# Queries and keys laid out before the launch, three half-height products per score, a shorter weight conversion, and new durations in the plan

## The chip, the cores and the metric

The kernel runs on one core of one Trainium2 chip. The metric is the device time of one execution in microseconds: the median of 3 runs is 1234.06 us (1233.96 to 1236.8). The core has five engines that run beside each other, each in the order of its own queue: TensorE (PE in the rows, its weight loads PEld), VectorE (DVE), ScalarE (ACT), GpSimd (POOL) and SyncE (SP), which here only issues DMA transfers.

## The reference, cut to what matters

```python
def _attn_ref(q, k, v):            # (4, 8, 576, 64) each: batch, heads, rows, width
    scores = scale * np.matmul(q, k.transpose(0, 1, 3, 2))
    kth = np.partition(scores, -32, axis=-1)[..., -32:-31]
    scores = np.where(scores >= kth, scores, -1e9)     # only the 32 largest of a row stay
    attn = softmax(scores)
    return np.matmul(attn, v)
x = attn_out.transpose(0, 2, 1, 3).reshape(2304, 512)
x = ((x @ w_a) * (x @ w_b)) @ w_out                    # 512 -> 1536 -> 512, "MoE 1" in the code
logits = x @ w_gate                                    # 8 experts
out[rows of expert e] = gate[:, None] * (np.maximum(x @ w1[e], 0) @ w2[e])   # each row to one expert
```

`w_a`, `w_b` and `w_out` arrive as 8-byte floats; everything else has 4 bytes.

## The kernel before

The kernel has three parts that overlap. Attention runs over 4 batches and 4 pairs of heads. Batch 0 is taken in two halves of its rows (320 and 256 of the 576), so it has 8 units (pair, half); batches 1 to 3 have 4 units each, 12 in all, the "later units". The feed-forward `moe1` follows for each half or batch, and after the last batch the 8 experts.

**Units.** `load_unit` brings q, k and v of one unit in, rows on partitions, and `prep_unit` turns q and k so that the head's 64 columns lie on partitions. In batch 0 (`u.f`) the turned operands stay f32: TensorE transposes at L488 and L491, ScalarE copies out of PSUM at L498 to L503, and a score (L597, and L572 for the last 64 rows of both heads) is an f32 matmul per head with 64 rows of contraction. In the later units q and k are first split into two float32r parts, a rounded one and the rest (ScalarE at L512, GpSimd at L514). The two parts of one head lie on 64 partitions each, so that one matmul of 128 rows computes high by high plus low by low, and a second one with a copy of k whose halves are swapped (`kS`, a transfer of 304 KB in two issues at L542) the mixed products. The turning is 18 transposes a unit at L523 and copies at L528 to L540. A score over one chunk of 128 rows and half of the keys has two heads by two products (L601); the score of the last 64 rows of both heads has eight matmuls (L578).

**Selection.** ScalarE copies half of the scores out of PSUM (L606), VectorE takes the larger and the smaller of the two halves (`m`, `n`, L614), and finds the 32 largest by rounds of MAX8 and MATCH_REPLACE8 (L625 to L652). ScalarE does the exponentials (L633), VectorE masks and sums (L680), TensorE turns the result (L706, L715) and multiplies it by v (L727, L731).

**Conversion.** `conv` makes a 4-byte float out of each 8-byte one by arithmetic on its two words, in 36 pieces of 128 x 512: ScalarE L387 (magnitude), VectorE L389 (shift and mask), ScalarE L391 (sign), VectorE L392 (shift and or), GpSimd L395 (times the sign). `split` (L400, L401) then makes two float32r parts, and these go to DRAM (`ws`, `wos`), from where `moe1` reads them (L824, L854: three products each). The first two pieces are loaded at once; the others wait for `U[0].mark`, which was the last copy of the first unit's preparation.

**Order.** Nothing is issued in program order. `Plan` holds each operation with an engine, a reckoned duration and a position `pos`; `emit` simulates the engines with these durations and issues each engine's operations in the order in which the simulation started them, the ready one with the smallest `pos` first. Attention has small positions, `moe1` large ones, so feed-forward matmuls fill TensorE where attention leaves it free. The durations are the functions `c_act`, `c_dve`, `c_ts`, `c_pool`, `c_mm` and `c_dma` and some numbers at the call. SP issues the loads and stores in the plan's order too.

Of the kernel before, what the change touches and what calls it, by code (L numbers as in the profile page):

```python
# [13 lines left out]
U32 = mybir.dt.uint32  # L14
AF = mybir.ActivationFunctionType
# [181 lines left out]
def c_pool(n):  # L197
    return 150 + n * 2.1


def c_mm(n, k=1):
    return k * (max(n, 256) / 2.4 + 2.5)
# [7 lines left out]
def fused_kernel(ctx: ExitStack, tc: tile.TileContext, q, k, v, w_a, w_b, w_out, w_gate, w1, w2, out,  # L210
                 opts=None, dbg=None):
    nc = tc.nc
# [18 lines left out]
    HALVES = opts.get("halves", (0,))  # L231
    FU = opts.get("fu", range(8))
# [74 lines left out]
    qm_t, rr_t = [], []  # L307
    for i in range(2):
        qm_t.append(cst.tile([128, 192], F32R, name=f"qm{i}"))
        nc.gpsimd.memset(fr(qm_t[i]), 0.0)  # L310
    for i in range(opts.get("rr", 1)):
        rr_t.append(cst.tile([128, 5, 128], F32, name=f"rr{i}"))
        nc.gpsimd.memset(rr_t[i], 0.0)
    id2 = cst.tile([128, 64], F32, name="id2")
# [14 lines left out]
    QM = [P_.fixed(t) for t in qm_t]  # L329
# [27 lines left out]
    def conv_bufs():  # L357
# [74 lines left out]
    def load_unit(ui, b, p, groups, pos, after=None):  # L432
        u = Rec()
        u.b, u.p, u.f, u.first = b, p, ui in FU, ui == 0
        ch = [x - x // 3 for g in groups for x in GT[g] if x != 2]
        u.c = min(ch), max(ch) + 1, any(2 in GT[g] for g in groups)
        h0 = 2 * p
# [6 lines left out]
        for nm, src in (("k", k), ("q", q)):  # L444
            z = T(p_at, [128, 10, 64], F32, "raw" + nm, opts.get("raw", 1))
            u.raw[nm] = z
            if u.f:
                a, e, last = u.c if nm == "q" else (0, 4, True)
                for h in range(2):
                    load(c_dma(65536 * (e - a)), pos, lambda z=z, h=h, a=a, e=e: z()[:, h + 2 * a:h + 2 * e - 1:2, :],  # L450
                         src[b, h0 + h, 0:512, :].rearrange("(p c) d -> p c d", c=4)[:, a:e], [(z, h)])
                if last:
                    load(c_dma(65536), pos, lambda z=z: z()[0:64, 8:10, :],
                         src[b, h0:h0 + 2, 512:576, :].rearrange("h s d -> s h d"), [(z, 2)])
                continue
            load(c_dma(262144), pos, lambda z=z: z()[:, 0:8, :].rearrange("p (h c) d -> p h c d", h=2),
                 src[b, h0:h0 + 2, 0:512, :].rearrange("h (p c) d -> p h c d", c=4), [(z, 0)])
            for h in range(2):
                load(c_dma(16384), pos, lambda z=z, h=h: z()[64 * h:64 * h + 64, 8, :], src[b, h0 + h, 512:576, :],
                     [(z, 1 + h)])  # L460
        z = T(p_at, [128, 2, 5, 64], F32, "vt", opts.get("vt", 2))
        vp = 40 if u.first else pos + 1
        load(c_dma(262144), vp, lambda: z()[:, :, 0:4, :],
             v[b, h0:h0 + 2, 0:512, :].rearrange("h (p c) d -> p h c d", c=4), [(z, 0)])
        for h in range(2):
            load(c_dma(16384), vp, lambda h=h: z()[64 * h:64 * h + 64, h, 4, :], v[b, h0 + h, 512:576, :], [(z, 1 + h)])
        u.vt = z
        return u

    def prep_unit(u, i, pos, step):  # L470
        u.qm, u.rr = QM[i % 2], RR[i % len(RR)]
# [1114 lines left out]
```

## Time and profile before

| | |
|---|---|
| median of 3 runs | 1234.06 us |
| profiled execution, its time | 1233.15 us |
| its span, first to last instruction | 1231.4 us |
| PE busy | 1103.6 us, 90%, 7710 matmuls |
| PEld busy | 981.2 us, 80% |
| DVE busy | 896.3 us, 73%, 2636 instructions |
| ACT busy | 718.1 us, 58%, 1567 |
| POOL busy | 460.6 us, 37%, 622 |
| DMA moved | 215.49 MB in 116863 packets, 28883 of them under 512 B |

Busy is the time in which an engine had an instruction in it. Matmuls are pipelined: a row's duration holds the time to fill and empty the array, and what a matmul costs in a stream is the distance from its start to the next one's start. Rows that follow each other with the same line and shape are merged in the timeline, with their count.

### The profile page before, as it was taken

How to read it: one execution, taken by the hardware profiler on the slowest of the kernel's cores; microseconds unless marked ns; L12 is line 12 of the kernel's file. 1: busy time of each engine (PE TensorE's matmuls, PEld its weight loads, DVE VectorE, ACT ScalarE, POOL GpSimd, SP SyncE). 2: the span in 40 equal slices, each digit the busy share in tenths (PEclk: the TensorE clock that was granted, in tenths of full speed). 3: DMA queues.
4: the chain of work that ended last, by engine and by line, in shares of the span. 5: the costliest groups of instructions: out<-in, count | busy, mean ns of one | idle time of the engine just before them, and what ended most of it. 6: DMA issues, size and time to landing. Idle time of an engine off the chain costs nothing.

```text
span 1231.4 us, 22514 instructions
## 1 busy us (share of the span) xinstructions
PE 1103.6 (90%) x7710; PEld 981.2 (80%) x7710; DVE 896.3 (73%) x2636; ACT 718.1 (58%) x1567; POOL 460.6 (37%) x622
## 2 busy tenths in 40 slices
PE   4656796979999789999999999999999999999996
PEld 2333474868888579889888998989999899999996
DVE  6999999999998999999998999910004545444441
ACT  6667676776667567666765766633224445544551
POOL 3455566755536234234535422455234100000001
PEclk9966798989999999999999999999899999999998
DMA  8487578999677234244243442246535655554450
GB/s 235 130 276 229 164 245 261 323 303 300 208 255 248 93 87 144 109 153 144 78 152 112 132 151 104 86 155 225 191 147 184 189 152 174 176 177 151 159 177 22
DMA packets 116863, 215.49 MB, mean 175 GB/s; under 512 B 28883, under 2 KB 77011, under 8 KB 109061
## 3 DMA queue, kind: packets, MB, share of 16 engines
q1 hardware_dynamic: 113525, 204.52, 52.4%
q0 software_dynamic: 3216, 9.46, 2.0%
q8 instruction: 63, 1.03, 0.4%
q14 instruction: 59, 0.48, 0.1%
HBM read 171.82 MB, written 35.25 MB: 168 GB/s over the span
## 4 chain that ended last, share of the span: by engine, by line
PE 55%; DVE 14%; DMA 11%; issue 8%; ACT 7%; POOL 4%; SPq 1%; POOLq 0%; ACTq 0%; DVEq 0%
PE ab L824 16%; PE ab L854 9%; PE ab L1182 5%; PE pv L727 5%; DVE am L680 3%; DVE m L638 3%; PE ms L1231 3%; PE pv L1231 3%; PE sp L601 3%; DVE kt L641 2%; PE tp L706 2%; DMA xsort<-rows,pi 2%; DMA rawk<-in_k_dram 2%; DMA wt<-wos 1%; PE pv L731 1%
## 5 line engine op out<-in xcount | busy, mean ns | idle before, releaser
L824 PE MATMUL ab<-xh,wt 128*128 128x320 f32 (+1 forms) x1344 | 303.9, 304 | 3.9 <-ACT sb L809 3.8
L824 PEld LDWEIGHTS ab<-xh,wt 128*128 128x128 f32 x1344 | 227.6, 191 | 13.2 <-issue 7.8
L824 PE MATMUL ab<-xl,wt 128*128 128x320 f32 (+1 forms) x672 | 199.9, 297 | 0.0
L638 DVE MATCH_REPLACE8 m<-kt,m 128x288 f32<-128x288 f32 x432 | 188.5, 440 | 0.0
L641 DVE MAX8 kt<-m 128x8 f32<-128x288 f32 x432 | 182.3, 444 | 0.5
L854 PE MATMUL ab<-gH,wt 128*128 128x320 f32 (+1 forms) x768 | 171.8, 305 | 4.5 <-DMA wt<-wos 4.5
L680 DVE SCALAR_TENSOR_TENSOR am<-s,kt,e 128x576 f32<-128x576 f32 x144 | 139.8, 996 | 0.3
L854 PEld LDWEIGHTS ab<-gH,wt 128*128 128x128 f32 x768 | 130.7, 193 | 6.7 <-DMA wt<-wos 3.9
L832 POOL TENSOR_TENSOR sa<-sa,sb 128x320 f32<-128x320 f32 (+1 forms) x96 | 79.6, 829 | 145.0 <-ACT sb L809 144.5
L824 PEld LDWEIGHTS ab<-xl,wt 128*128 128x128 f32 x672 | 128.8, 192 | 0.0
L633 ACT ACTIVATE e<-s,nm 128x576 f32<-128x576 f32 x144 | 108.6, 778 | 11.6 <-POOL nm L628 11.3
L854 PE MATMUL ab<-gT,wt 128*128 128x320 f32 (+1 forms) x384 | 115.1, 300 | 0.0
L1256 POOL DMA_INDIRECT out_dram<-y,ti x23 | 23.0, 999 | 227.6 <-ACT y L1250 212.6
L1100 DVE TENSOR_TENSOR wp<-raw,wp 128x1024 fp32r<-128x1024 f32 (+1 forms) x73 | 67.4, 942 | 55.6 <-ACT wp L1099 55.2
L606 ACT COPY s<-sp 128x576 f32<-128x576 f32 x128 | 81.9, 640 | 42.9 <-PE sp L601 23.7
L706 PE MATMUL tp<-idr,am 128*128 128x128 f32 x512 | 84.8, 304 | 20.3 <-ACT aT L710 7.2
L401 POOL TENSOR_TENSOR gT<-sa,gH 128x320 fp32r<-128x320 f32 (+1 forms) x96 | 84.6, 881 | 45.8 <-ACT gH L400 45.4
L706 PEld LDWEIGHTS tp<-idr,am 128*128 128x128 f32 x512 | 64.1, 155 | 38.6 <-ACT aT L710 15.8
L1182 PE MATMUL ab<-xgh,wp 128*128 128x304 f32 (+6 forms) x352 | 89.4, 312 | 1.1 <-DVE gT L1189 0.7
L710 ACT COPY aT<-tp 128x512 f32<-128x512 f32 x128 | 72.4, 587 | 26.6 <-PE tp L706 25.8
L727 PE MATMUL pv<-aT,vt 128*64 128x320 f32 (+1 forms) x512 | 79.2, 451 | 6.5 <-ACT aT L695 4.5
L809 ACT ACTIVATE sa<-ab 128x320 f32<-128x320 f32 (+1 forms) x120 | 49.4, 412 | 53.9 <-PE ab L824 30.7
(303 smaller groups left out, 2560.8 us busy)
## 6 DMA issues: line engine op xcount, KB each, us to landing
wt<-ws SPq DMA_DIRECT2D x54, 1024.0 KB, 5.6
wt<-wos SPq DMA_DIRECT2D x44, 768.0 KB, 5.7
raw<-in_moe_w_dram SPq DMA_DIRECT2D x64, 512.0 KB, 3.7
kS<-kT SPq DMA_DIRECT2D x24, 304.0 KB, 4.5
xsort<-rows SPq DMA_DIRECT2D x8, 771.0 KB, 14.4
wp<-ws SPq DMA_DIRECT2D x6, 1024.0 KB
vt<-in_v_dram SPq DMA_DIRECT2D x20, 256.0 KB, 3.1
gT<-in_moe_w_a_dram SPq DMA_DIRECT2D x8, 512.0 KB, 4.1
```

The costliest lines, as they stand in the source:

```text
L401: P(POOL, c_pool(cost), pos, lambda: nc.gpsimd.tensor_sub(lo(), src(), fr(hi())), r=rd + wh, w=wl)
L606: P(ACT, c_act(S), pos, lambda hf=hf, sp=sp: nc.scalar.copy(s()[:, :, hf * HS:(hf + 1) * HS], sp()[:, :, 0:HS]), r=[sp], w=[(s, (h, hf)) f ...
L633: P(ACT, c_act(S, True) + 90, pos, lambda h=h, e=e: nc.scalar.activation(e(), s()[:, h], AF.Exp, bias=nm()[:, h], scale=SCALE), r=[(s, (h, ...
L638: P(DVE, c_dve(HS), pos + 5.0 * h, lambda x=x, h=h, j=j: nc.vector.match_replace(out=m()[:, h], in_to_replace=kt(j, 8 * x - 8, 8 * x), in_ ...
L641: P(DVE, c_dve(HS), pos + 5.0 * h, lambda x=x, h=h, j=j: nc.vector.max(out=kt(j, 8 * x, 8 * x + 8), in_=m()[:, h]), r=[(m, h)], w=[KT(j, x)])
L680: P(DVE, c_dve(S) + 60, pos, lambda: nc.vector.scalar_tensor_tensor(am(), sc(), kth(), e(), op0=OP.is_ge, op1=OP.mult, accum_out=r.sum()[: ...
L706: res = nc.tensor.transpose(tp()[:, 512 * h + x * 128:512 * h + (x + 1) * 128], z()[:, 640 * h + x * 128:640 * h + (x + 1) * 128], idf)
L727: nc.tensor.matmul(pv()[64 * h:64 * h + 64, 0:n], u.vt()[:, h, j, :], r.aT[h]()[:, j, 0:n], start=(j == 0), stop=False)
L824: res = nc.tensor.matmul(pa()[:, 0:n], view()[:, m, wi, ko, :], xv()[:, ko], start=(ko == 0 and x == 0), stop=(ko == KO - 1 and x == 2))
L832: P(POOL, c_pool(n), pos, lambda: nc.gpsimd.tensor_mul(sa()[:, 0:n], sa()[:, 0:n], sb()[:, 0:n]), r=[sb], w=[sa])
L854: res = nc.tensor.matmul(pa()[:, 0:n], wv()[:, wi, f, :], gv()[:, f, :], start=(f == 0 and x == 0), stop=(f == HB - 1 and x == 2))
L1182: res = nc.tensor.matmul(pa()[:, 0:cap], p1[ko]()[:, wi, f * 128:(f + 1) * 128], xv()[:, ko], start=(ko == 0 and i == 0), stop=(ko == KO - ...
```

## The change

The numpy function `lay_out` is called by `kernel()` before the launch. It passes q and k with a head's 64 columns on the partitions, two heads above each other, and v in one block per pair; the original arrays are still passed for the fallback at the end of the program. `load_unit` then needs one transfer each for q, k and v (the first unit: three for k, two for q). In batch 0 the loaded tiles are used as they are. In the later units they are split into two float32r parts, and a score is three products per head (high by high, low by high, high by low) with 64 rows of contraction; the score of the last 64 rows uses a q laid out with zeros, so that three products of 128 rows serve both heads. The raw tiles have two buffers instead of one. `U[0].mark` becomes a load. The conversion has three ScalarE steps, one GpSimd step and one VectorE step. The durations in the plan are new.

```diff
 def c_act(n, sbuf=False):
-    return (95 if sbuf else 55) + n * 0.83
+    return (140 if sbuf else 90) + n * 0.83
 def c_dve(n, psum=False):
-    return (n + (100 if psum else 66)) / 0.96
+    return (n + (80 if psum else 66)) / 0.96
 def c_ts(n):
-    return (n / 2 + 66) / 0.96
+    return (n / 2 + 66) / 0.96 + 200
 def c_pool(n):
-    return 150 + n * 2.1
+    return 170 + n * 2.25
 def c_mm(n, k=1):
-    return k * (max(n, 256) / 2.4 + 2.5)
+    return k * (max(n, 256) / 2.4 + 13.5)
...
-        P(ACT, c_act(CW, True), pos, lambda: nc.scalar.activation(f(), hi(), AF.Abs, scale=2.0 ** -111),
+        def top():
+            return raw().bitcast(U8).rearrange("p (n t) -> p n t", t=8)[:, :, 3]
+        P(ACT, c_act(CW, True), pos, lambda: nc.scalar.activation(f(), hi(), AF.Relu, scale=-2.0 ** -79),
           r=[(zr, "r")], w=[(zf, fk)])
-        P(DVE, c_ts(CW), pos, lambda: nc.vector.tensor_scalar(
-            fi(), fi(), 3, 0x7fffffff, op0=OP.logical_shift_left, op1=OP.bitwise_and), w=[(zf, fk)])
-        P(ACT, c_act(CW, True), pos, lambda: nc.scalar.activation(hi(), hi(), AF.Sign), w=[(zr, "r")])
-        P(DVE, c_dve(CW), pos, lambda: nc.vector.scalar_tensor_tensor(
-            fi(), words(0), 29, fi(), op0=OP.logical_shift_right, op1=OP.bitwise_or),
+        P(ACT, c_act(CW, True), pos, lambda: nc.scalar.activation(
+            words(0), top(), AF.Relu, scale=2.0 ** -5, bias=cut),
+          w=[(zr, "r")])
+        P(ACT, c_act(CW, True), pos, lambda: nc.scalar.activation(hi(), hi(), AF.Relu, scale=2.0 ** -111), w=[(zr, "r")])
+        P(POOL, c_pool(CW), pos, lambda: nc.gpsimd.tensor_add(f(), f(), hi()), r=[(zr, "r")], w=[(zf, fk)])
+        P(DVE, c_dve(CW) + 170, pos, lambda: nc.vector.scalar_tensor_tensor(
+            fi(), fi(), 3, words(0), op0=OP.logical_shift_left, op1=OP.bitwise_or),
           r=[(zr, "r")], w=[(zf, fk)], label=f"cv{nconv[0]}")
-        P(POOL, c_pool(CW), pos, lambda: nc.gpsimd.tensor_mul(f(), f(), hi()), r=[(zr, "r")], w=[(zf, fk)])
...
+        for nm, src, n in (("k", kx, 640), ("q", qx, 640)):
+            z = T(p_at, [128, n], F32, "raw" + nm, opts.get("raw", 2))
+            u.raw[nm] = z
+            cut = [0, n]
+            if u.first:
+                cut = [0, 64, 64 + HS, n] if nm == "k" else [0, 128, n]
+            for c0, c1 in zip(cut, cut[1:]):
+                u.mark = load(c_dma(512 * (c1 - c0)), pos + (c0 == 0 and u.first and nm == "k"),
+                              lambda z=z, c0=c0, c1=c1: z()[:, c0:c1], src[b, p, :, c0:c1], [(z, c0)])
+        u.vt = T(p_at, [128, S], F32, "vt", opts.get("vt", 2))
+        load(c_dma(294912), 40 if u.first else pos + 1, lambda: u.vt(), vx[b, p], [u.vt])
...
         if u.f:
+            u.q, u.k = [u.raw["q"]], [u.raw["k"]]
             return
+        for ni, nm in enumerate("kq"):
+            raw = u.raw[nm]
+            n = 640
+            p0 = pos + 3 * ni * step
+            hi = T(p_at, [128, n], F32R, nm + "H", opts.get("kS", 2))
+            lo = T(p_at, [128, n], F32R, nm + "L", opts.get("kS", 2))
+            P(ACT, c_act(n, True), p0, lambda raw=raw, hi=hi: nc.scalar.copy(hi(), raw()), r=[raw], w=[hi])
+            P(POOL, c_pool(n), p0, lambda raw=raw, hi=hi, lo=lo: nc.gpsimd.tensor_sub(lo(), raw(), fr(hi())),
+              r=[raw, hi], w=[lo])
...
+    def products(u):
+        return [(u.q[0], u.k[0])] if u.f else [(u.q[0], u.k[0]), (u.q[1], u.k[0]), (u.q[0], u.k[1])]
...
                 def score(hf=hf, sp=sp):
+                    pr = products(u)
+                    for x, (qp, kp) in enumerate(pr):
+                        for h in range(2):
+                            a, k0 = slice(64 * h, 64 * h + 64), 0 if h else 64
+                            res = nc.tensor.matmul(sp()[:, h, 0:HS], qp()[a, c * 128:(c + 1) * 128],
+                                                   kp()[a, k0 + hf * HS:k0 + (hf + 1) * HS], start=(x == 0),
+                                                   stop=(x == len(pr) - 1))
                     return res
-                P(PE, 780 if u.f else c_mm(HS, 4), pos, score, r=[u.qT, u.kT] + ([] if u.f else [u.kS]), w=[sp],
+                P(PE, 780 if u.f else 540, pos, score, r=u.q + u.k, w=[sp],
...
-            P(PE, 980 if u.f else c_mm(HS, 8), pos, score, r=[u.qT, u.kT] if u.f else [u.qm, u.kT, u.kS], w=[sp],
+            P(PE, 980 if u.f else 900, pos, score, r=u.q + u.k, w=[sp],
...
-                P(DVE, c_dve(HS), pos + 5.0 * h, lambda x=x, h=h, j=j: nc.vector.match_replace(
+                P(DVE, c_dve(HS) + 60, pos + 5.0 * h, lambda x=x, h=h, j=j: nc.vector.match_replace(
...
-            P(DVE, c_dve(S) + 60, pos, lambda: nc.vector.scalar_tensor_tensor(
+            P(DVE, c_dve(S) + 310, pos, lambda: nc.vector.scalar_tensor_tensor(
```

The diff also has an option `g1f` (which half of a batch comes first) and code for the last batch taken in halves; with the options as they are, neither is used.

## Rows read from the trace of the kernel before

**Rows 1.** The page: TensorE, VectorE and the rest busy; DMA and its rate in 40 slices.
```profile
PE 1103.6 (90%) x7710; PEld 981.2 (80%) x7710; DVE 896.3 (73%) x2636; ACT 718.1 (58%) x1567; POOL 460.6 (37%) x622
...
DMA  8487578999677234244243442246535655554450
GB/s 235 130 276 229 164 245 261 323 303 300 208 255 248 93 87 144 109 153 144 78 152 112 132 151 104 86 155 225 191 147 184 189 152 174 176 177 151 159 177 22
```

**Rows 2.** Busy time by stage: stage, length, PE, PEld, DVE, ACT, POOL, clock, DMA, GB/s.
```profile
0.00:147.00 147.00, 88.22 (x363) 51.63 (x363) 133.23 (x392) 98.75 (x202) 73.84 (x104) 0.79 0.70 207
147.00:229.00 82.00, 66.00 (x420) 52.20 (x416) 80.95 (x226) 59.77 (x125) 52.65 (x54) 0.92 0.85 263
229.00:425.00 196.00, 175.01 (x1319) 154.85 (x1319) 184.27 (x591) 134.56 (x312) 98.92 (x134) 0.98 0.76 248
425.00:800.00 375.00, 362.60 (x2736) 327.44 (x2737) 352.31 (x1135) 246.87 (x570) 142.18 (x211) 0.99 0.37 119
800.00:1231.00 431.00, 411.73 (x2878) 395.08 (x2876) 145.57 (x296) 178.15 (x363) 92.97 (x123) 0.98 0.50 163
```

**Rows 3.** Timeline (start, length): last attention row of VectorE, last batch's first feed-forward.
```profile
800.44 1.42 DVE L680 SCALAR_TENSOR_TENSOR am<-s,kt,e 128x576 f32<-128x576 f32 x1
...
825.36 0.41 PE L824 MATMUL ab<-xh,wt 128*128 128x320 f32 x1
```

**Rows 4.** VectorE's L389, its sum up to 308 us; timeline of one and its follower.
```profile
0.00:308.00 308.00, 21.17 (x36) 0.87 0.81 247
...
51.96 0.40 DVE L389 TENSOR_SCALAR gH<-gH 128x512 int32<-128x512 int32 x1
52.29 0.81 DVE L680 SCALAR_TENSOR_TENSOR am<-s,kt,e 128x576 f32<-128x576 f32 x1
```

**Rows 5.** Groups of ScalarE up to 308 us: busy, mean ns; idle before, releaser.
```profile
L387 ACT ACTIVATE gT<-gT 128x512 f32<-128x512 f32 x11 | 7.4, 675 | 6.0 <-DMA gT<-in_moe_w_a_dram 3.3 <-DMA gT<-in_moe_w_out_dram 2.4 <-issue 0.3
...
L503 ACT COPY kT<-tp 128x576 f32<-128x576 f32 (+2 forms) x9 | 5.4, 597 | 4.2 <-PE tp L491 4.2
...
L503 ACT COPY qT<-tp 128x256 f32<-128x256 f32 x7 | 2.7, 380 | 0.2 <-PE tp L488 0.2
```

**Rows 6.** Timeline of TensorE at the start: first transposes, first score.
```profile
4.83 1.09 PE L488 MATMUL tp<-idr,rawk 128*128 128x128 f32 x4 [4.83 <-DMA rawk<-in_k_dram]
...
7.71 1.33 PE L597 MATMUL sp<-kT,qT 64*128 64x288 f32 x4 [0.58 <-ACT qT L503]
```

**Rows 7.** Timeline of TensorE: a group of five transposes of a later unit.
```profile
485.34 0.55 PE L523 MATMUL tp<-idr,hl 128*128 128x128 f32 x5
485.73 0.38 PE L824 MATMUL ab<-xh,wt 128*128 128x320 f32 x1
485.94 0.31 PE L824 MATMUL ab<-xl,wt 128*128 128x320 f32 x1
```

**Rows 8.** Timeline of TensorE: a score of a later unit (four matmuls) and its follower.
```profile
489.69 0.30 PE L601 MATMUL sp<-kT,qT 128*128 128x288 f32 x1
...
490.22 0.28 PE L824 MATMUL ab<-xh,wt 128*128 128x256 f32 x1
```

**Rows 9.** Timeline of TensorE: an f32 score of batch 0 between feed-forward matmuls.
```profile
171.52 0.31 PE L824 MATMUL ab<-xh,wt 128*128 128x320 f32 x1
171.76 0.76 PE L597 MATMUL sp<-kT,qT 64*128 64x288 f32 x4
172.44 0.41 PE L824 MATMUL ab<-xh,wt 128*128 128x320 f32 x1
172.69 0.31 PE L824 MATMUL ab<-xl,wt 128*128 128x320 f32 x1
```

**Rows 10.** Timeline of TensorE: products with v, two heads in turn, 256 columns.
```profile
805.26 1.95 PE L727 MATMUL pv<-aT,vt 128*64 128x256 f32 x16
807.14 0.65 PE L731 MATMUL pv<-aTt,vt 64*64 64x256 f32 x4
```

**Rows 11.** VectorE's waits from 308 to 800 us: total, times, longest.
```profile
DVE m L614 <- ACT s L606: 13.4, 9, 3.4
```

More of the change, by code (lines that the diff above doesn't have):

```diff
@@ L14 @@
 U32 = mybir.dt.uint32
+U8 = mybir.dt.uint8
 AF = mybir.ActivationFunctionType
@@ L306, in fused_kernel @@
     nc.gpsimd.memset(wg, 0.0)
[L307 to L310, printed above, removed]
+    rr_t = []
     for i in range(opts.get("rr", 1)):
@@ L442, in load @@
                 o.deps.add(after)
-        for nm, src in (("k", k), ("q", q)):
-            z = T(p_at, [128, 10, 64], F32, "raw" + nm, opts.get("raw", 1))
+            return o
+        for nm, src, n in (("k", kx, 640), ("q", qx, 640)):
+            z = T(p_at, [128, n], F32, "raw" + nm, opts.get("raw", 2))
             u.raw[nm] = z
[L447 to L467, printed above, removed]
+            cut = [0, n]
+            if u.first:
+                cut = [0, 64, 64 + HS, n] if nm == "k" else [0, 128, n]
@@ L472, in prep_unit @@
[L472 to L473 removed]
+        u.rr = RR[i % len(RR)]
         if u.f:
[L475 to L505 removed]
@@ L730, in av @@
                 a = slice(64 * h, 64 * h + 64)
-                res = nc.tensor.matmul(pv()[a, 0:n], u.vt()[a, h, 4, :], r.at()[a, 0:n], start=False, stop=True)
+                res = nc.tensor.matmul(pv()[a, 0:n], u.vt()[a, 512:576], r.at()[a, 0:n], start=False, stop=True)
             return res
@@ L785, in moe1 @@
         xx = {}
+        if b == B - 1 and groups == (1,):
+            ranks()
+            first_rows()
         for g in groups:
@@ L886, in moe1 @@
                     marks.append(P_.ops[-1])
-                    if b == 0 and groups == (0,) and hf == 1 and not opts.get("fo", 0):
+                    if b == 0 and groups == ((1,) if 0 in G1F else (0,)) and hf == 1 and not opts.get("fo", 0):
                         for x in range(fi * E // HB, (fi + 1) * E // HB):
@@ L905, in moe1 @@
                 marks.append(P_.ops[-1])
+        if b == B - 1 and groups == (1,):
+            gating(b, x2, groups, fill, ["xh1", "xl1"], True)
+            return
         gating(b, x2, groups, fill)
@@ L1309, in fused_kernel @@
     for b in range(B):
-        sets = [(g,) for g in (0, 1)] if b in HALVES else [(0, 1)]
+        sets = [(g,) for g in ((1, 0) if b in G1F else (0, 1))] if b in HALVES else [(0, 1)]
         for groups in sets:
@@ L1564, with lay_out, main, last @@
 _INS = ["q", "k", "v", "moe_w_a", "moe_w_b", "moe_w_out", "moe2_w_gate", "moe2_w1", "moe2_w2"]
+_LAID = ["qx", "kx", "vx"]
 _OUT = ((2304, 512), "float32")
+def lay_out(q, k, v):
+    import numpy as np
+    B, H, S, D = q.shape
+    def main(a):
+        return a[:, :, 0:512].reshape(B, H, 128, 4, D).transpose(0, 1, 4, 3, 2).reshape(B, H, D, 512)
+    def last(a):
+        return a[:, :, 512:S].transpose(0, 1, 3, 2)
+    ql = np.zeros((B, H // 2, 2, D, 2, S - 512), q.dtype)
+    for h in range(2):
+        ql[:, :, h, :, h] = last(q)[:, h::2]
+    qx = np.concatenate([main(q).reshape(B, H // 2, 2 * D, 512), ql.reshape(B, H // 2, 2 * D, 128)], axis=3)
+    kx = np.concatenate([last(k), main(k), last(k)], axis=3).reshape(B, H // 2, 2 * D, S + 64)
+    vm = v[:, :, 0:512].reshape(B, H // 2, 2, 128, 4, D).transpose(0, 1, 3, 2, 4, 5).reshape(B, H // 2, 128, 8 * D)
+    vx = np.concatenate([vm, v[:, :, 512:S].reshape(B, H // 2, 128, D)], axis=3)
+    return {"qx": qx, "kx": kx, "vx": vx}
 def kernel(**inputs):
@@ L1574 @@
     arrays, args = {}, []
-    for name in _INS:
-        a = np.ascontiguousarray(inputs[name])
+    given = {**inputs, **lay_out(inputs["q"], inputs["k"], inputs["v"])}
+    for name in _INS + _LAID:
+        a = np.ascontiguousarray(given[name])
         if a.dtype == np.float64:
```

122 lines of the change are left out of this document (22 added, 100 removed).

## The prediction

> **What bounds the kernel now.** I read the busy shares first, then the busy times by stage, and only then single rows, because the shares mix stages. TensorE is busy for 90% of the span and VectorE for 73% [rows 1]; the stages part the two [rows 2]. Up to 147 us VectorE works 133 of 147 us and TensorE only 88, at a granted clock of 0.79: there is no expert or feed-forward work yet, only attention and the conversion of the weights. From 147 to 229 us VectorE has 1 us idle in 82. From 425 to 800 us both are full: VectorE idles 23 us of 375, TensorE 12. After 800 us only TensorE counts (412 of 431 us). The hand-over shows how closely the two are matched: the last attention row on VectorE starts at 800.44 us, and the feed-forward of the last batch starts on TensorE at 825.36 [rows 3]. So about 25 us of older TensorE work is then still in hand, and from 825.36 to the end TensorE needs 406 us, which the change does not touch. The end therefore moves by what VectorE gains in the first two batches, provided that TensorE's own work does not grow.
>
> **1. The conversion (36 times).** Of two VectorE steps one goes: the TENSOR_SCALAR at L389, 21.17 us in 36 [rows 4]. Where it runs alone it shows 0.40 us and its follower starts 0.33 us after it, so the 36 hold the engine for some 21.2 - 36 x 0.07 = 18.7 us, the long ones included. VectorE has no cover in this stage, so this counts in full: -18.7 us, about 16 of them before 229 us. Bounds: 36 x 0.33 = 12 us, and 21.2. On ScalarE a step is added: two ACTIVATEs become three, 36 x 0.675 = +24.3 us [rows 5]. One of them reads every eighth byte, which no row shows; the two old ones already read and write every second word and take the same 0.675, so I take that for it, with 0.6 and 1.3 (twice) as ends. It is covered as long as ScalarE has room: 158.5 us busy up to 229 us [rows 2]. Part 2 takes 9 us off there, the new step puts 21 on, so it would be about 170 of 211 us, 81%. Without that cover VectorE would wait for the score copies; the upper price alone would add 23 us of ScalarE, still under the stage. POOL's multiplication becomes an addition of the same shape: 0.
>
> **2. Loads already turned, units of batch 0.** The transposes and their copies go. At the start the chain load, transposes, copies, score runs from 4.83 to the first score at 7.71 us [rows 6]; it becomes load, score. That is -2.9 us, but the first unit now brings 655 KB of k and q instead of some 450, and all of it is waited for: +0.9 us at the 235 GB/s of the first slice [rows 1]. I take -2 us, between 0 and -4. Later the ScalarE copies removed (9 x 0.597 + 7 x 0.38 us and small ones, about 10 us, [rows 5]) and the transposes on TensorE lie beside VectorE's work and count nothing.
>
> **3. Later units (12), TensorE.** 18 transposes a unit go, in four groups. A group of five occupies TensorE from 485.34 to 485.73, and the matmul after it costs 0.21 instead of 0.15 [rows 7]: 0.45 us a group, 1.8 a unit, -21.6 us. The score of the unit with both heads' last rows goes from eight matmuls to six; both forms are of full height, so two steps of 0.133 fall away, -0.27 x 12 = -3.2 us. The other scores (8 a unit, 96 in all) go from four products of full height, 489.69 to 490.22 = 0.53 us or 0.133 a step [rows 8], to six of half height. That form of float32r is not in the trace. The nearest row is the f32 score of batch 0, which also uses half the array's height per head [rows 9]: its matmuls start 0.24 us after the one before, hold TensorE 0.68 us, and the one after them takes 0.25; less 0.15 for each neighbour's own step that is 0.87 us. I read its four records as two pairs, the heads of a pair running together; f32 records of 256 columns that stand in pairs take 1.88 us for eight pairs [rows 10], so 0.26 a pair at 288 columns, 0.53 for two. About 0.35 us is then the price of going into and out of the half-height form. Three overlapped pairs of float32r give 3 x 0.133 + 0.35 = 0.75 us, +0.22 each, +21 us in all. Ends: 0.40 (no price, -12.5 us in all) and, if the halves do not overlap, 6 x 0.133 + 0.35 = 1.15 (+60 us). I take 0.75, the row's. The sum on TensorE is -21.6 - 3.2 + 21 = about -4 us: nothing that the end would show.
>
> The rule that this part leans on is in the Trainium skill, TensorEngine Tiling (Array Packing), section Theoretical Speedup: a contraction of 64 or less can run up to twice as fast in tiles. By it alone the 96 scores would save 12.5 us. The same page, section Key Properties, says that a change of tiling mode drains TensorE; the 0.24 and 0.25 us on either side of the f32 score agree with that, and the measured rows decide for 0.75 us here.
>
> **4. Later units, the rest.** ScalarE loses the copies out of PSUM, and the transfer that swaps k's halves goes with its issues on SP. VectorE's waits for the score copies are 13.4 us between 308 and 800 us [rows 11]; they are what this can shorten. Ends 0 and -13.4; I take -3, because VectorE only gains where TensorE, equally full, keeps pace. POOL's subtractions grow from 576 to 640 columns; POOL works 142 of 375 us there [rows 2]: 0.
>
> **5. The plan's new durations** change the order on all engines. What that is worth can be bounded only by what it could remove, VectorE's idle 23 us from 425 to 800 [rows 2], and by a like amount lost through a worse order. I take 0.
>
> **Sum.** -18.7 - 2 - 3 = -23.7 of the span of 1231.4: 1207.7 us. The profiled execution took 1233.15, 1.75 more than its span, so 1209.5; the median of the runs, 1234.06, is 0.9 above it: **1210 us**. TensorE must follow. Up to 425 us it idles 59 + 16 + 21 = 96 us [rows 2]; a shift of 21 us needs only that it loses 21 of these, and the first stage, shorter by 13 us, gives back most of them.
>
> **Rivals.**
> (a) *The halves do not overlap*: float32r at half height runs one product after the other, 1.15 us a score. For: no row shows float32r in this form, and that the f32 records overlap is my reading of merged rows. Against: four f32 records one after the other, each as long as a pair's 0.26, would take 1.04 us without any price at the edges, and the row has 0.87 with them. From 425 us on TensorE is full, so this goes on the end: 60 - 25 on TensorE against -23.7 + 3 early: +14, about 1248 us. It is slower than before from a score of about 1.0 us on.
> (b) *The early gain is lost to transfers.* From 229 to 425 us DMA is busy 76% of the time, and the slices from 215 to 308 us show 9 tenths and more [rows 1]. If the loads of weights there keep their old time, VectorE's lead turns into TensorE idling and some 5 us remain: 1229 us. Against: the swap transfers and loads in 256-byte rows go.
> (c) *The full stage loosens too*: better durations and an idler ScalarE remove 12 of VectorE's 23 idle us and TensorE's 25 us of work in hand shrinks by as much: 1198, at best 1185.
> (d) *The new order is worse*: the plan counts a score with 540 ns where I have 0.75 us, 96 x 0.2 = 20 us of delay that it does not know; if VectorE waits for all of it, 1210 + 20 = 1230, and with the 23 us bound of part 5 1233; some of it lies above 1238.
>
> **How the numbers follow.** Forecast 0.49 (1203 to 1222), (c) 0.17, (b) 0.13, (a) 0.11, (d) 0.10. A measurement of this kernel can tell about 0.3%, 3.7 us. Faster: the forecast, (c) and three quarters of (b), 0.76; same: the rest of (b) and half of (d), 0.08; slower: (a) and the other half of (d), 0.16. The range leaves out the far ends of (a) and (c): 1185 to 1240.
>
> **What would show it.** Right: the last attention row of VectorE at about 777 us instead of 800; no TENSOR_SCALAR in the conversion, ScalarE's share up to 229 us near 80%; the first score near 6 us; later scores in pairs 7 to 10 ns apart, 0.7 to 0.8 us from neighbour to neighbour; TensorE's busy sum nearly unchanged after 425 us. Wrong: scores over 1 us, VectorE idle growing in the first 229 us behind ScalarE or POOL, or an unchanged stretch from 229 to 425 us with more TensorE idling.

## The result, and the profile after

The changed kernel takes **1219.4 us** (median of 4 runs, 1217.3 to 1223.1) against 1234.0 us before: ratio 0.9886, interval 0.985 to 0.9921. The forecast was 1210, range 1185 to 1240. The time fits the range, but the terms behind it do not: one was far too large, one far too small, and one that was taken as nothing costs almost as much as the whole change gains. The experiments below part them. The profiled execution has a span of 1215.6 us (before: 1231.4), so the traces differ by 15.8 us, and their readings are of that size.

The page of the kernel after, part 1 (answers to the first line of [rows 1]):
```profile
PE 1087.7 (89%) x7586; PEld 944.2 (78%) x7586; DVE 884.6 (73%) x2600; ACT 702.5 (58%) x1478; POOL 467.0 (38%) x621
```
VectorE lost 12 us of work where the forecast removed 19, TensorE lost 16. By stage, as in [rows 2] (stage, length, PE, PEld, DVE, ACT, POOL, clock, DMA, GB/s):
```profile
0.00:147.00 147.00, 81.30 (x315) 48.15 (x315) 131.49 (x377) 107.43 (x208) 78.71 (x106) 0.78 0.72 226
147.00:229.00 82.00, 66.26 (x401) 51.80 (x402) 77.70 (x217) 62.05 (x122) 57.48 (x55) 0.86 0.82 275
229.00:425.00 196.00, 175.55 (x1301) 147.48 (x1301) 183.99 (x599) 127.55 (x282) 95.44 (x131) 0.94 0.67 230
425.00:800.00 375.00, 367.98 (x2795) 318.27 (x2792) 344.17 (x1104) 231.44 (x519) 151.81 (x221) 1.00 0.32 110
800.00:1215.60 415.60, 396.60 (x2782) 378.50 (x2780) 147.25 (x307) 174.07 (x352) 83.52 (x110) 0.99 0.50 165
```
In the full stage, 425 to 800 us, VectorE idles more than before (31 us instead of 23) and TensorE less (7 instead of 12). The hand-over, as in [rows 3] (start, length):
```profile
803.33 0.82 DVE L611 SCALAR_TENSOR_TENSOR am<-s,kt,e 128x576 f32<-128x576 f32 x1
```
```profile
812.12 0.42 PE L758 MATMUL ab<-xh,wt 128*128 128x320 f32 x1
```
VectorE's last attention row, forecast at about 777 us, came *later* than before (803.33, was 800.44). The last batch's feed-forward came 13 us earlier all the same, since TensorE's work in hand between the two fell from 25 to 9 us. So what was gained came over TensorE; VectorE's lead did not come. From the end of batch 0 (229.3 us before, 225.6 after) to its last attention row VectorE is busy 537 us before and 535 after (533 to 540 in every kernel here but two_full); what differs is how long it idles there, 34.4 us before and 42.8 after.

A later score (answers to [rows 8]; two heads' halves are merged into one row x2):
```profile
490.17 0.40 PE L531 MATMUL sp<-kH,qH 64*128 64x288 f32 x2
490.41 0.30 PE L531 MATMUL sp<-kH,qL 64*128 64x288 f32 x2
490.54 0.29 PE L531 MATMUL sp<-kL,qH 64*128 64x288 f32 x2
490.76 0.39 PE L758 MATMUL ab<-xh,wt 128*128 128x256 f32 x1
490.98 0.28 PE L758 MATMUL ab<-xl,wt 128*128 128x256 f32 x1
```
The heads of a pair mostly start within 10 ns of each other, so they overlap; the middle pair takes 0.13 us, the first and last 0.24 and 0.22, and the follower 0.22 instead of 0.12. Less the neighbours' own steps, 40 such scores held TensorE 0.79 us (median). The form costs 0.79 - 3 x 0.133 = 0.39 us to enter and leave. That a change of tiling mode drains TensorE is what the Trainium skill says (TensorEngine Tiling (Array Packing), Key Properties); the rows agree and put the price to it, which the page doesn't give.

The start (answers to [rows 6]): the first score waits for nothing but its loads.
```profile
3.86 1.29 PE L531 MATMUL sp<-rawk,rawq 64*128 64x288 f32 x2 [3.86 <-DMA rawq<-in_qx_dram]
```
VectorE's waits from 308 to 800 us (answers to [rows 11]; total, times, longest):
```profile
DVE m L545 <- ACT s L537: 10.4, 6, 2.8
DVE sum L683 <- POOL sum L681: 8.0, 7, 3.8
DVE xf L711 <- PE pv L700: 6.9, 7, 1.8
```
The conversion on ScalarE (answers to [rows 5]; groups up to 308 us: busy, mean ns; idle before):
```profile
L394 ACT ACTIVATE gH<-gH,cut 128x512 int32<-128x512 uint8 x11 | 8.4, 766 | 0.0
...
L392 ACT ACTIVATE gH<-gH 128x512 f32<-128x512 f32 x11 | 7.4, 676 | 4.1 <-DMA gH<-in_moe_w_b_dram 4.1
```
The step on every eighth byte takes 0.77 us where the others take 0.68. No TENSOR_SCALAR is left ([rows 4]). But VectorE's attention rows became longer, and the timeline shows beside what (VectorE, then POOL, same stretch):
```profile
21.55 0.96 DVE L399 SCALAR_TENSOR_TENSOR gT<-gT 128x512 int32<-128x512 int32 x1
22.43 1.85 DVE L611 SCALAR_TENSOR_TENSOR am<-s,kt,e 128x576 f32<-128x576 f32 x1
```
```profile
21.92 1.74 POOL L398 TENSOR_TENSOR x<-x,xl 128x512 f32<-128x512 f32 x1
23.62 1.79 POOL L407 TENSOR_TENSOR gT<-gT 128x512 fp32r<-128x512 f32 x1
```
An attention row takes 0.80 us with no POOL work beside it, and 1.85 here, ending 0.6 us after the POOL step that it met. In batch 0, 27 of 36 rows meet POOL and take 1.35 us on average; the other 9 take 0.80. Of the 27, 19 began when the POOL instruction had more than 0.3 us still to run, and each of these ended 0.61 to 0.62 us after it: the row stood still until POOL was done.

### The profile page after: what moved, and what is told of

The parts are those of the page before. It is cut to its first block, busy times and chain, and to the rows that moved or that the text cites. A ratio compares the mean times of both kernels' runs of the same rounds, so it can differ in the third digit from the quotient of the medians.

```text
span 1215.6 us, 21852 instructions
## 1 busy us (share of the span) xinstructions
PE 1087.7 (89%) x7586; PEld 944.2 (78%) x7586; DVE 884.6 (73%) x2600; ACT 702.5 (58%) x1478; POOL 467.0 (38%) x621
## 4 chain that ended last, share of the span: by engine, by line
PE 52%; DVE 16%; issue 10%; DMA 9%; ACT 7%; POOL 4%; SPq 0%; POOLq 0%; DVEq 0%; ACTq 0%
PE ab L758 18%; PE ab L788 11%; PE pv L658 4%; PE ab L1119 4%; DVE m L569 4%; PE sp L531 3%; DVE am L611 3%; DVE kt L572 3%; PE tp L637 3%; DMA raw<-in_moe_w_dram 2%; DMA xsort<-rows,pi 2%; PE pv L1168 1%; DMA gT<-in_moe_w_a_dram 1%; DMA out_dram<-y,ti 1%; PE pv L662 1%
## 5 line engine op out<-in xcount | busy, mean ns | idle before, releaser
L611 DVE SCALAR_TENSOR_TENSOR am<-s,kt,e 128x576 f32<-128x576 f32 x144 | 146.1, 1043 | 0.1
L766 POOL TENSOR_TENSOR sa<-sa,sb 128x320 f32<-128x320 f32 (+1 forms) x96 | 83.7, 872 | 148.1 <-ACT sb L743 141.6
L788 PEld LDWEIGHTS ab<-gH,wt 128*128 128x128 f32 x768 | 128.4, 190 | 10.2 <-issue 8.3
L407 POOL TENSOR_TENSOR gT<-sa,gH 128x320 fp32r<-128x320 f32 (+1 forms) x96 | 80.9, 843 | 44.7 <-ACT gH L406 44.4
L537 ACT COPY s<-sp 128x576 f32<-128x576 f32 x128 | 81.6, 638 | 25.0 <-PE sp L531 18.7
L531 PE MATMUL sp<-rawk,rawq 64*128 64x288 f32 x128 | 39.1, 681 | 56.5 <-ACT s L537 14.9
```

What stands on the lines that cost most here:

```text
L407: P(POOL, c_pool(cost), pos, lambda: nc.gpsimd.tensor_sub(lo(), src(), fr(hi())), r=rd + wh, w=wl)
L537: P(ACT, c_act(S), pos, lambda hf=hf, sp=sp: nc.scalar.copy(s()[:, :, hf * HS:(hf + 1) * HS], sp()[:, :, 0:HS]), r=[sp], w=[(s, (h, hf)) f ...
L611: P(DVE, c_dve(S) + 310, pos, lambda: nc.vector.scalar_tensor_tensor(am(), sc(), kth(), e(), op0=OP.is_ge, op1=OP.mult, accum_out=r.sum()[ ...
L766: P(POOL, c_pool(n), pos, lambda: nc.gpsimd.tensor_mul(sa()[:, 0:n], sa()[:, 0:n], sb()[:, 0:n]), r=[sb], w=[sa])
L788: res = nc.tensor.matmul(pa()[:, 0:n], wv()[:, wi, f, :], gv()[:, f, :], start=(f == 0 and x == 0), stop=(f == HB - 1 and x == 2))
```

## The experiments

One table serves most of them: the end of batch 0's attention on VectorE, VectorE's last attention row, the start of the last batch's feed-forward on TensorE, and the span. The two ends of attention are given as starts of the last row; from the last feed-forward to the end it is 401 to 406 us in all but one of the kernels (415 in lay_dve), so **the column "last feed-forward" decides**. "Its before" is the kernel before, timed along with the run; ratios are to it. Between runs with different "before" times a difference of medians and a difference of ratios can disagree by 1 to 3 us, and both are given where that matters.

| kernel | median us (its before) | batch 0 ends | last row | last feed-forward | span |
|---|---|---|---|---|---|
| before | 1234.0 | 229.3 | 800.4 | 825.4 | 1231.4 |
| after | 1219.4 | 225.6 | 803.3 | 812.1 | 1215.6 |
| conv_alone | 1237.5 (1233.6) | 218.4 | 800.7 | 831.6 | 1236.0 |
| dur_alone | 1240.8 (1233.6) | 232.8 | 818.9 | 834.2 | 1239.6 |
| layout_alone | 1207.7 (1233.6) | 225.4 | 788.7 | 803.8 | 1207.6 |
| all_but_conv | 1228.8 (1233.6) | 232.3 | 813.3 | 822.1 | 1227.0 |
| all_but_dur | 1206.1 (1232.2) | 222.6 | 785.5 | 800.6 | 1203.4 |
| two_full | 1244.7 (1232.2) | 229.0 | 821.7 | 838.6 | 1243.4 |
| lay_dve | 1250.9 (1232.2) | 234.1 | 841.0 | 834.6 | 1249.2 |
| after_score790 | 1224.5 (1232.2) | 224.8 | 796.6 | 818.1 | 1223.8 |
| abd_other | 1217.1 (1234.2) | 224.6 | 774.6 | 809.1 | 1212.0 |
| fast_dve | 1237.4 (1234.2) | 225.6 | 774.7 | 831.3 | 1232.4 |
| no_low | 1208.6 (1234.2) | 217.2 | 785.1 | 803.1 | 1206.9 |
| four | 1217.1 (1234.2) | 222.3 | 798.1 | 813.3 | 1215.2 |

**conv_alone: the new conversion in the kernel before.**
```diff
 # conv(): TENSOR_SCALAR and Sign out; Relu on the byte, third Relu, POOL add in
-        P(DVE, c_ts(CW), pos, lambda: nc.vector.tensor_scalar(fi(), fi(), 3, 0x7fffffff, ...
+        P(ACT, c_act(CW, True), pos, lambda: nc.scalar.activation(words(0), top(), AF.Relu, ...
```


> The kernel before with the new conversion of the weights alone. Observed after the whole change: the last attention row of batch 0 came 3.7 us earlier on VectorE (229.3 to 225.6 us), not the 16 us forecast, and the rows of attention (am) had become longer there (1.01 to 1.21 us on average). Theory L (the removed step had been waiting for POOL; the waiting passes to the steps that stay): the same 3 to 6 us at the end of batch 0, am again at 1.15 us or more, whole kernel 1228 to 1232 us. Rival O (the step was worth its full 16 us, and the new order of the work or the turned layout took it back): batch 0 ends at 211 to 216 us, am stays at 1.0 us, whole kernel 1215 to 1222 us.


Ratio 1.0029 (1.0015 to 1.0043). Neither theory is right: batch 0 ended 10.9 us earlier, more than theory L allowed and less than O, and nothing of it is left at the end. From batch 0's end to the last row VectorE idles 42.7 us instead of 34.4 and works 2.9 us longer, 11.2 in all. In batch 1 the lead is spent waiting for scores (VectorE's waits from 225 to 440 us: total, times, longest; in the kernel before the first kind took 5.5 us there, the second 1.1):
```profile
DVE m L621 <- ACT s L613: 9.5, 5, 4.2
DVE m L621 <- PE sp L608: 4.4, 1, 4.4
```
In the longest of these VectorE stops at 351.6 us; TensorE meanwhile does feed-forward matmuls and transposes, and the score comes after them:
```profile
353.80 0.40 PE L861 MATMUL ab<-gH,wt 128*128 128x256 f32 x2
354.04 0.28 PE L861 MATMUL ab<-gT,wt 128*128 128x256 f32 x1
354.16 0.28 PE L861 MATMUL ab<-gH,wt 128*128 128x256 f32 x1
354.28 1.03 PE L713 MATMUL tp<-idr,am 128*128 128x128 f32 x8
355.07 0.38 PE L608 MATMUL sp<-kT,qT 128*128 128x288 f32 x1
```
```profile
355.95 0.76 DVE L621 TENSOR_TENSOR m<-sp,s 128x576 f32<-128x576 f32 x1 [4.36 <-PE sp L608]
```
Another 3.6 us, at the turn from batch 0 to batch 1, the profile puts down to a DMA: a loss of the kind of rival (b), and the smaller part.

**dur_alone: the new durations in the kernel before.**
```diff
-    return (n / 2 + 66) / 0.96
+    return (n / 2 + 66) / 0.96 + 200
 # and c_act, c_dve, c_pool, c_mm, match_replace +60, attention row +310, as in the change
```


> The kernel before with the plan's new durations alone (scores keep their c_mm cost). Theory L: the order matters for TensorE's idle time of the full stage only; batch 0 ends within 2 us of 229.3, whole kernel 1226 to 1234 us. Rival O: the new order holds VectorE up, batch 0 ends at 234 us or later, whole kernel 1238 us or more.


Ratio 1.0063 (1.0042 to 1.0083): slower. Batch 0 ends 3.5 us later, between the two theories' figures, and the last row 18.5 us later; the time is rival O's.

**layout_alone: turned q, k, v and three products, old conversion, old durations.**
```diff
 # the changed kernel with before's conv(), before's c_act ... c_mm and match_replace, +60 on the attention row
```


> The kernel before with q, k and v laid out turned and three products per later score, old conversion, old durations (M and N scores planned with 900 and 540 ns). Theory L: this is where most of the gain is: batch 0 ends 2 to 4 us earlier, TensorE idles some 5 us less from 417 us on, whole kernel 1222 to 1228 us. Rival O: the layout costs as much in batch 0 as it gives later, batch 0 ends at 232 us or later, whole kernel 1230 to 1236 us.


Ratio 0.9788 (0.9771 to 0.9805): better than the whole change, and than either theory. The stages to the second batch's feed-forward, to the last batch's, and to the end, of before and of this kernel (columns as in [rows 2]):
```profile
0.00:417.00 417.00, 324.76 (x2071) 254.67 (x2071) 390.45 (x1184) 289.23 (x629) 222.78 (x284) 0.90 0.77 240
417.00:825.40 408.40, 392.28 (x2959) 354.36 (x2957) 363.24 (x1166) 259.00 (x599) 160.26 (x237) 0.99 0.37 120
825.40:1231.40 406.00, 386.54 (x2688) 372.18 (x2684) 142.64 (x288) 169.86 (x340) 77.51 (x103) 0.98 0.50 164
```
```profile
0.00:409.70 409.70, 307.64 (x1947) 235.62 (x1948) 388.86 (x1174) 267.34 (x558) 219.26 (x281) 0.87 0.74 245
409.70:803.80 394.10, 386.92 (x2958) 334.25 (x2956) 363.55 (x1175) 241.31 (x546) 165.28 (x238) 1.00 0.33 111
803.80:1207.60 403.80, 386.08 (x2688) 371.40 (x2684) 142.66 (x288) 169.73 (x340) 77.40 (x103) 0.98 0.50 165
```
The first part is 7.3 us shorter, the full stage 14.3, the tail 2.2. Of the 14.3, TensorE's busy time gives 5.4 and its idle time 8.9 (16.1 to 7.2). Most of the 5.4 is the granted clock and not the work. In the kernel before, TensorE was busy for 4.65 of the 8.5 us up to 425.5, and then the granted clock fell to 0.5, its lower level of 1.2 GHz, from 425.5 to 432.3 and again from 439.1 to 442.5 us; in layout_alone it stays at 1.00 (2.4 GHz) throughout the stage. Before first, then layout_alone:
```profile
417.00:425.50 8.50, 4.65 (x31) 4.19 (x30) 8.50 (x27) 3.85 (x8) 2.62 (x6) 1.00 0.17 64
425.50:432.30 6.80, 6.12 (x29) 4.49 (x30) 6.80 (x25) 4.35 (x9) 1.31 (x3) 0.50 0.00 0
```
```profile
425.50:432.30 6.80, 5.94 (x45) 5.46 (x45) 6.80 (x23) 4.67 (x10) 1.74 (x4) 1.00 0.16 45
```
A feed-forward matmul of 320 columns follows the one before it after 0.267 us at the lower level and 0.147 at the upper (medians). TensorE was busy for 9.4 us of the two stretches, so at the upper level the same work would have taken about 4.2 us less, an estimate from these rows. From batch 0's end to the last row VectorE idles 26.7 us, 7.7 less than before.

**all_but_conv: the change with the old conversion.**
```diff
 # the changed kernel; conv() as before
```


> The changed kernel with the old conversion put back. Theory L: the conversion is worth 2 to 6 us: 1221 to 1226 us, am in batch 0 back to about 1.0 us. Rival O: it is worth 12 us or more: 1231 us and above.


Ratio 0.9967 (0.9951 to 0.9984). The same conversion that was worth nothing in conv_alone is worth 9 us here, on top of the new durations: between the two theories.

**all_but_dur: the change with the old durations.**
```diff
 # the changed kernel; c_act, c_dve, c_ts, c_pool, c_mm, match_replace, attention row, conversion's STT as before
```


> The changed kernel with the plan's old durations put back (scores keep 540 and 900 ns): new layout and new conversion together. So far: the layout alone takes 1207.7 us, the conversion alone 1237.5, the new durations alone 1240.8. Theory A (parts add): 1207.7 + 3.9 = 1210 to 1213 us. Theory I (the conversion is worth nothing only because VectorE's lead from batch 0 is spent waiting for score copies in batch 1; with fewer copies on ScalarE the lead stays): batch 0 ends at 214 us, batch 1 near 407, whole kernel 1196 to 1202 us.


Ratio 0.9796 (0.9767 to 0.9825). Its interval lies below the change's own (0.985 to 0.9921): without the new durations the kernel is some 11 to 13 us faster. It is the fastest median of the study, though not told from layout_alone. The time lies between the two theories, 4 us from either: below what A's sum gives, so the conversion cost nothing here, and above I's, with batch 0 ending at 222.6 instead of 214. The full stage of this kernel:
```profile
414.50:800.60 386.10, 383.61 (x2937) 332.46 (x2935) 354.52 (x1147) 237.11 (x537) 163.85 (x234) 1.00 0.33 114
```
TensorE idles 2.5 us in 386. Against the change (413.7 to 812.1, 398.4 us, TensorE 388.75 busy) 7.2 of 12.3 us are idle time and 5.1 busy time, of nearly the same instructions. The change had 6.8 us of the lower clock in this stage, all of them busy, and this kernel none: by the same two steps that is about 3 of the 5.1.

**four: TensorE's load raised in the same order.**
```diff
-        return [(u.q[0], u.k[0])] if u.f else [(u.q[0], u.k[0]), (u.q[1], u.k[0]), (u.q[0], u.k[1])]
+        return [(u.q[0], u.k[0])] if u.f else [..., (u.q[0], u.k[1]), (u.q[1], u.k[1])]
```


> Layout and conversion with the old durations (1206.1 us), with the fourth product (low times low) added to each later score, at the same planned cost and in the same order: by 0.133 us for a pair of heads +12.8 us on TensorE for 96 scores and 2 x 0.133 x 12 = +3.2 for the rows of both heads. Theory T (TensorE, idle 1.3 us a batch in batches 2 and 3, sets the end): +12 to +16 us, 1218 to 1222. Rival V (VectorE sets it, TensorE has slack): 1206 to 1211 us.


10.9 us more by the medians (1206.1 to 1217.1), 7.6 by the ratios (0.9796 to 0.9858, 0.9834 to 0.9883). The planned costs are the same, and in the traces VectorE, ScalarE and POOL run the same instructions in the same order, TensorE too but for the added products, so the test is clean. TensorE's busy time over the whole span rose by 15.4 us (1083.6 to 1099.0), the span by 11.8: theory T in kind, with half to three quarters of its size. Its full stage:
```profile
420.30:813.30 393.00, 392.41 (x3072) 342.53 (x3069) 355.06 (x1144) 237.21 (x537) 164.94 (x234) 1.00 0.33 112
```
TensorE idles 0.6 us; VectorE, with the same work in the same order, ends 12.6 us later. TensorE is the bound of this stage in this order.

**two_full: TensorE's load lowered.**
```diff
+                hi = T(p_at, [128, 2, 640], F32R, nm + "H", 2)   # raw loaded into both halves
+                nc.scalar.copy(hi(), raw())                       # 1280 columns
+                nc.gpsimd.tensor_sub(hi()[64:128], raw()[64:128], fr(hi()[64:128]))
+                nc.sync.dma_start(sw()[64*a:64*a+64], hi()[64-64*a:128-64*a])   # halves swapped
```


> The kernel with the new layout alone (1207.7 us), but each later score as two products of full height again, high and low parts stacked: q and k come in loaded into both halves, k's halves are swapped by a transfer inside the chip. No transposes. A score should hold TensorE 0.53 us instead of 0.79, so 96 x 0.26 less, and the 12 scores of last rows 0.27 more: -22 us on TensorE. ScalarE and POOL work on 1280 columns instead of 640 per tensor: POOL some +35 us in all. Theory T (TensorE sets the full stage): VectorE's last row stays near 788 us, the last feed-forward starts 12 to 15 us earlier than 803.8, then VectorE limits; 1192 to 1198 us. Rival V (VectorE, slowed by POOL, sets it): last row of VectorE at 795 us or later, 1205 to 1213 us.


Slower than before, 1.01 (1.0072 to 1.0128): worse than rival V's own figure. Scores fell to 0.53 us as meant:
```profile
351.70 0.30 PE L548 MATMUL sp<-kH,qH 128*128 128x288 f32 x1
351.83 0.29 PE L548 MATMUL sp<-kS,qH 128*128 128x288 f32 x1
351.96 0.30 PE L548 MATMUL sp<-kH,qH 128*128 128x288 f32 x1
352.10 0.29 PE L548 MATMUL sp<-kS,qH 128*128 128x288 f32 x1
352.23 0.28 PE L774 MATMUL ab<-xh,wt 128*128 128x256 f32 x1
```
But VectorE's last row came at 821.7 instead of 788.7. Its attention rows in batch 1 rose from 0.98 to 1.21 us beside POOL's wider subtractions (POOL 461.9 to 500.0 us in all). From batch 0's end to the last row VectorE is busy 554.8 us instead of 536.6 and idles 37.9 instead of 26.7, so the larger part of its delay is longer instructions. TensorE idled 19.7 us in the full stage instead of 7.2. Both engines bind, and the load taken off one was put where it delays the other. The order changed as well, and from 226 to 430 us TensorE waited 6.1 us for weights from DRAM beside the added transfers; the price of each isn't parted here.

**lay_dve, fast_dve, abd_other: the pace of VectorE in the plan.**
```diff
 # lay_dve = layout_alone with VectorE's new durations only (c_dve, c_ts, match_replace +60, row +310)
 # fast_dve = all_but_dur with
-            P(DVE, c_dve(S) + 60, pos, ...        # attention row
+            P(DVE, c_dve(S) - 190, pos, ...       # and c_dve(HS) - 60 for match_replace
 # abd_other = all_but_dur with the new c_act, c_pool, c_mm
```


> The kernel with the new layout alone (1207.7 us) and of the new durations only VectorE's (c_dve, c_ts, +60 for match_replace, +310 for the attention row). All new durations together bring the layout kernel to 1228.8 us, with batch 1 of attention ending at 430.9 instead of 418.3 us. Theory W (a plan with a slower VectorE places the scores later in TensorE's order, and VectorE waits for them): 1222 to 1230 us, batch 1 ends at 428 us or later. Rival E (the durations of the other engines do it): 1205 to 1211 us, batch 1 within 3 us of 418.

> Layout and conversion with the old durations (1206.1 us), but VectorE counted faster than before: the attention row with 250 ns less than the old figure, match_replace with 60 less. Theory W (pace of VectorE against the others in the plan): 1190 to 1204 us, VectorE's waits for score copies under 8 us in all. Rival N (just another order): 1206 to 1230 us.

> Layout and conversion with the old durations took 1206.1 us; this adds the new durations of ScalarE, POOL and TensorE (c_act, c_pool, c_mm) and leaves VectorE's old. VectorE's new durations alone, added to the layout, cost 43 us (1250.9), all of them together 21 (1228.8). Theory W (a plan that counts VectorE too slow against the others places scores late; the other durations made up for half of it): 1185 to 1204 us, VectorE idle before its last attention row under 40 us. Rival N (any new set of durations gives just another order, with no direction): between 1206 and 1230 us.


lay_dve: ratio 1.0155 (1.0127 to 1.0184), 43 to 45 us worse than layout_alone. fast_dve: 1.0026 (1.0007 to 1.0045), 28 to 31 us worse than all_but_dur. abd_other: 0.9864 (0.984 to 0.9888), 8 to 11 us worse. Theory W fails as a direction: both kernels that it said would gain lost. abd_other's 1217.1 is what rival N (just another order) said; fast_dve's 1237.4 lies above both, and lay_dve's 1250.9 far above W's 1230. What holds of W is that the planned pace of VectorE sets where it waits. VectorE's largest wait for score copies over the whole attention (total, times, longest), lay_dve first:
```profile
DVE m L544 <- ACT s L536: 26.9, 17, 3.4
```
```profile
DVE gb L893 <- PE ms L885: 53.4, 2, 50.1
...
DVE m L545 <- ACT s L537: 4.7, 4, 3.8
```
A VectorE planned slow does wait for scores; its last row comes at 841.0, after the last feed-forward could begin. Planned fast it waits little and ends at 774.7, but then waits 50 us for TensorE, which has done the scores first and has 57 us of feed-forward left:
```profile
774.66 0.81 DVE L611 SCALAR_TENSOR_TENSOR am<-s,kt,e 128x576 f32<-128x576 f32 x1
```
```profile
831.27 0.41 PE L758 MATMUL ab<-xh,wt 128*128 128x320 f32 x1
```
The three fastest kernels, layout_alone, all_but_dur and no_low, have 15 to 18 us in hand there. Kernels with more in hand are slower than these (57, 34.5, 31, 25 us), and so is the one with none (-6). The number alone is no recipe: dur_alone and two_full have 15 to 17 as well, with VectorE late, and abd_other, with 34.5, is no slower than the change with 9.

**after_score790: the plan told what a score costs.**
```diff
-                P(PE, 780 if u.f else 540, pos, score, ...
+                P(PE, 780 if u.f else 790, pos, score, ...
```


> The changed kernel (1219.4 us), with the later scores counted in the plan with 790 ns, as they were measured, instead of 540. Theory W (the loss is in the new durations of VectorE): 1215 to 1224 us, no clear difference. Rival S (the loss comes from the plan not knowing what the scores cost): 1205 to 1213 us, VectorE's waits for score copies from 225 to 440 us fall by half.


Ratio 0.9931 (0.991 to 0.9953), against the change's 0.9886 (0.985 to 0.9921): no gain. VectorE's waits for score copies there fell from 5.6 to 3.2 us, and the last feed-forward came 6 us later. Right figures in the plan didn't help.

**no_low: POOL's subtraction out of the conversion.**
```diff
-        split(CW, f, lambda: hl()[:, 0], lambda: hl()[:, 1], ...)
+        P(ACT, c_act(CW, True), pos, lambda: nc.scalar.copy(hl()[:, 0], f()), ...)
 # the low parts are stored from a constant tile of zeros
```


> Layout and conversion with the old durations (1206.1 us), without POOL's subtraction that makes the weights' low parts: 36 times some 1.3 us of POOL go; the low parts of w_a, w_b and w_out are stored as zeros from a constant tile, so that part of the weights is left out. Theory L (VectorE's attention rows wait for POOL: 0.80 us where no POOL work lies beside them, 1.41 where it does): the mean row of batch 0 falls from 1.29 to about 1.0 us, batch 0 ends 7 to 12 us before 222.6, whole kernel 1196 to 1204 us. Rival (the rows are long for another reason, such as ScalarE or DMA): mean row stays above 1.2 us, batch 0 within 3 us of 222.6.


The mean row of batch 0, all_but_dur first, then no_low:
```profile
L611 DVE SCALAR_TENSOR_TENSOR am<-s,kt,e 128x576 f32<-128x576 f32 x36 | 45.4, 1291 | 0.0
```
```profile
L613 DVE SCALAR_TENSOR_TENSOR am<-s,kt,e 128x576 f32<-128x576 f32 x36 | 34.6, 986 | 0.1
```
The mean fell as theory L said, 10.8 us in 36 rows; batch 0 ended 5.4 us earlier, less than its 7 to 12. The end did not move: 0.9798 (0.9772 to 0.9824) against 0.9796, where theory L said 1196 to 1204 us and 1208.6 were measured. From batch 0's end to the last row VectorE idles 32.6 us, in all_but_dur 24.3. This is the second kernel in which VectorE's early lead is bought and lost. Its plan has fewer steps and so another order, which may hide a few us either way.

## Why the prediction came near, and what failed in it

**The step that failed** is the one on which all else stood: "The end therefore moves by what VectorE gains in the first two batches, provided that TensorE's own work does not grow." conv_alone gained 10.9 us in batch 0 and lost 3.9 at the end; no_low gained 5.4 more and nothing at the end. The proviso failed, not in TensorE's work but in its order: "a shift of 21 us needs only that it loses 21 of these" 96 idle us. TensorE lost none of them in conv_alone: 92.8 idle us up to the second batch's feed-forward, 92.2 before. Its order is written by the plan; scores of batch 1 stand behind feed-forward matmuls, as the rows under conv_alone show, and VectorE runs up to them and waits.

**1. Conversion, -18.7 forecast.** Measured +3.9 alone, nothing that can be told on the layout with old durations (ratios 0.9788 and 0.9796), -9.4 with new ones. By batch 0's end 10.9 of the 16 forecast for then had come in conv_alone; part of the rest is waiting that the attention rows took over from the removed step: the 35 rows there took 35.4 us before, 39.4 in conv_alone, 41.8 in the change. [rows 4] showed it without my reading it: 21.17 us in 36 steps of 0.40 alone is 6.8 us of waiting. The Trainium skill (SBUF — State Buffer, SBUF: two separate sides) has the reason: a VectorE instruction with two inputs in SBUF and a GpSimd instruction that reads SBUF share a port pair, and whoever is second blocks for the other's whole length. The rows above agree (0.80 alone, 1.85 beside POOL, ends 0.61 to 0.62 us after POOL's), and in no_low, with POOL's work taken away, the mean row fell by 0.3 us. ScalarE's third step cost 0.77, inside its bounds (0.6 to 1.3), and its work up to 229 us was 169.5 us for a forecast of about 170. In the whole change VectorE also idled more in batch 0, 19.8 us for 14.8, which the prediction had named as a sign of being wrong; with the old durations (all_but_dur) it was 15.3.

**2 to 4. Layout, -5 forecast, -25.9 measured alone.** The prices read from rows were about right: the first score came 3.85 us earlier (forecast 2, at most 4); the halves overlap, 0.79 us a score for a forecast 0.75, so rival (a) is refuted. Two agreements are luck. The waits of [rows 11] fell from 13.4 to 10.4 us in the change, the 3 that I took, but VectorE's whole idle time after batch 0 rose by 8.4 us. And TensorE's busy time in the full stage fell by 5.4 in layout_alone and 3.5 in the change (forecast some 4), but at 0.79 us a score the sum of part 3 is nothing (-21.6 - 3.2 + 25), and some 4 of the 5.4 are the granted clock. The mis-sized term is the one put at "nothing that the end would show" and at -3 for waits. In layout_alone TensorE idles 8.9 us less in the full stage, and VectorE 7.7 less after batch 0; that and 3.9 us in batch 0 brought VectorE's last row 11.7 us forward. That the shorter chain from load to score is the reason is argued, not shown. It is rival (c), which I gave 0.17, by another road than VectorE's lead.

**5. Durations, 0 forecast, +11 to +13 measured** (1206.1 to 1219.4 by the medians, 0.9796 to 0.9886 by the ratios; +7 in the kernel before, +21 on the layout alone). The bound given, "a like amount lost through a worse order", was the right size; choosing its middle was not. Rival (d) named the loss, but its cause, the planned 540 ns, is refuted by after_score790.

So -18.7 - 5 + 0 should have read 0 - 26 + 13: the sum agreed because two errors of opposite sign met, and no run supports the way to it. What stays open: why one set of durations orders better than another. lay_dve, abd_other and fast_dve bound VectorE's planned pace from both sides, but the old set beat every other one tried, and no rule was found by which to choose it. For the same reason it isn't shown how much of layout_alone's 26 us is the layout itself and how much the order that the plan made of it: every kernel here but four has an order of its own, and durations alone moved the time by 7 to 45 us. Nor was the layout of batch 0 run apart from that of the later units; the split by stage is read from the traces alone.

## What to carry to other kernels

When two engines are both full in a later stage, an early lead of one is not a gain until the other's order can use it; price a change by what it does in the saturated stage. A planner's durations are tuning knobs, not facts: time a layout change and a change of durations apart, because here new figures ate half of a 26 us gain. A step whose mean is well above its undisturbed time is absorbing a wait, and removing it hands that wait to its neighbour.

## What the hardware showed that I had not expected

VectorE's attention row, 0.80 us alone, met POOL work in 27 of 36 cases in batch 0 and reached 1.85 us, ending 0.61 to 0.62 us after the POOL instruction that it had to wait for. Entering and leaving the half-height form costs 0.39 us a score, so three pairs of half height (0.79) are dearer on TensorE than four products of full height (0.53). ScalarE took 0.77 us to read every eighth byte as uint8, 0.09 more than to read every second word of f32. Two stretches at the lower granted clock, 10.2 us together, are worth about 4 us of TensorE's time in the kernel before and are gone in layout_alone.
